# Token mix, transposes and channel product 2 between two tiles: in two half-depth products at the same time instead of in the full array

## The chip, the cores and the metric

One core of one Trainium2 chip. The time is the device time of the kernel in microseconds. TensorE (PE) multiplies, VectorE (DVE) and ScalarE (ACT) read PSUM and compute elementwise, GpSimd (POOL) and SyncE (SP) mostly issue DMAs.

## The reference

A convolution over the last seven tokens with softmax weights for each head, then an MLP over tokens and one over channels, with 8 images of 4096 tokens by 192 channels, all float32:

```python
out = np.einsum('hk,bskhg->bshg', w, x_unf)         # 8 heads, 7 taps, causal
xt = x.transpose(0, 2, 1)
h = np.maximum(xt @ w_tok1, 0.0) @ w_tok2           # tokens: 4096 -> 256 -> 4096
u = x + h.transpose(0, 2, 1)
h2 = np.maximum(u @ w_ch1, 0.0) @ w_ch2             # channels: 192 -> 1536 -> 192
return u + h2
```

## The kernel before

The images are worked in five groups: `[0]`, `[1]`, `[2, 3]`, `[4, 5]`, `[6, 7]`. A group has 8 tiles of 512 tokens (four token blocks of 128). Every float32 operand is split into a high and a low part, and a product is made of three part products (high by high, high by low, low by high). In a group of two images each tile goes through these steps, in the order of the code:

- Channel product 1 of an image (`channel1`, line 926): 192 channels are three columns of 64, so the contraction is 64 deep. Two products with different output features run at the same time, one in array rows 0 to 63, one in rows 64 to 127. A pair takes two PSUM tiles. ScalarE (L965) and VectorE (L966) read both and make `hh` and `hl`, the high and low part of the hidden layer.
- Channel product 2 (`channel2` or `channel2_halves`): the contraction over 1536 hidden features goes in 12 chunks of 128. `channel2` (L1000, L1001) uses all 128 array rows, one PSUM tile for a token block, and VectorE reads it in two adds (L1004, L1005). `channel2_halves` (L983) splits each chunk into rows 0 to 63 and 64 to 127, with a PSUM tile for each half, and VectorE makes four adds that depend on each other (L989, L991).
- Hand-over to the next tile (`turn`), which stands at the last image of the tile only: after its channel product 1 comes the token mix of the next tile (`mix2`, L858 to L860, contraction over 256 hidden tokens, four blocks, one PSUM tile each, added to `u` by VectorE in L873), then half of channel product 2, then the transposes of the mixed tile (`transposed`, L886, three columns, four float32 transposes and one PSUM tile each; ScalarE's L888 and VectorE's L889 make the high and low part in `own`), then the other half of channel product 2. Two copies by ScalarE (L894) and a DMA on POOL's queue (L895) put the other half of the partitions into `other`.

Before the change, images without a hand-over take `channel2_halves`, those with one take `channel2`.

All these products write tiles of the pool `ps_x`, which has six PSUM tiles and hands them out in turn. In this case each tile n waits until tile n − 6 has been read.

The work of the next group (its convolution on VectorE, L636, and its first token product on TensorE, L721 to L723, the background products) is a list of items. The planner `Background` places them between the steps by written costs: `bg.fg(pe, dve, after)` adds the cost of a step on the two engines and then places the items that fit, and while `bg.tiled` is set, no item with TensorE work is placed. There is no other scheduler; each engine runs its instructions in the order of the code.

Of the kernel before, what the change touches and what calls it, by code (L numbers as in the profile page):

```python
# [8 lines left out]
F32 = mybir.dt.float32  # L9
F32R = mybir.dt.float32r  # L10
U32 = mybir.dt.uint32
AF = mybir.ActivationFunctionType
ALU = mybir.AluOpType
AX = mybir.AxisListType

GROUPS = [[0], [1], [2, 3], [4, 5], [6, 7]]
# [98 lines left out]
def conv_mixer_kernel(ctx: ExitStack, tc: tile.TileContext, x, weight, w_tok1, w_tok2, w_ch1, w_ch2, out):  # L115
    nc = tc.nc
    B, S, D = x.shape
# [4 lines left out]
    P = 128  # L122
    NJ = S // P
    KC = JT // P
    NF = FF // P
    D2 = P // 2
    ND = D // D2
    NP = NF // 2
    TJ = 4
    MJ = 2  # L130
    NT = NJ // TJ
    TT = TJ * P
# [5 lines left out]
    def f32(ap):  # L138
        return ap.bitcast(F32)
# [5 lines left out]
    ps_x = ctx.enter_context(tc.tile_pool(name="ps_x", bufs=6, space=bass.MemoryType.PSUM))  # L145
    ps_a = ctx.enter_context(tc.tile_pool(name="ps_a", bufs=1, space=bass.MemoryType.PSUM))
    bg = Background()
# [5 lines left out]
    ident = const.tile([P, P], F32, name="ident")  # L153
# [677 lines left out]
    def rows(v):  # L831
        return v.rearrange("p (c d) -> p c d", d=D2)

    def mix2(gi, q, t2, u, at_once=False):
        nb = len(GROUPS[gi])
        n = nb * D

        def lhs(kc, r, j):
            if gi:
                return t2[:, kc, r, j, :]  # L840
            a0 = ((q % 2) * TJ + j) * P
            return t2s[q // 2][:, kc, r, a0:a0 + P]

        for j in range(TJ):
            ps = ps_x.tile([P, TT], F32, name="ps_x")
            for kc in range(KC):
                a, z = kc == 0, kc == KC - 1
                wh, wl = lhs(kc, 0, j), lhs(kc, 1, j)
                hh, hl = h1[:, kc, 0, :n], h1[:, kc, 1, :n]
                if at_once:  # L850
                    nc.tensor.matmul(out=ps[:, :D], lhsT=wh, rhs=hh, start=a, stop=False)
                    nc.tensor.matmul(out=ps[:, :D], lhsT=wh, rhs=hl, start=False, stop=False)
                    nc.tensor.matmul(out=ps[:, :D], lhsT=wl, rhs=hh, start=False, stop=z)
                elif nb == 1:
                    nc.tensor.matmul(out=ps[:, :2 * D], lhsT=wh, rhs=h1[:, kc, :, :n], start=a, stop=False)  # L855
                    nc.tensor.matmul(out=ps[:, :D], lhsT=wl, rhs=hh, start=False, stop=z)
                else:
                    nc.tensor.matmul(out=ps[:, :n], lhsT=wh, rhs=hh, start=a, stop=False)  # L858
                    nc.tensor.matmul(out=ps[:, :n], lhsT=wh, rhs=hl, start=False, stop=False)  # L859
                    nc.tensor.matmul(out=ps[:, :n], lhsT=wl, rhs=hh, start=False, stop=z)  # L860
            bg.fg(570 if nb == 1 else 1040, 660 if nb == 1 else 600, 200)
            uj = u[:, j]
            one, two = uj[:, :, 1], uj[:, :, 0]
            if at_once:
                nc.vector.tensor_tensor(out=two, in0=rows(ps[:, :D]), in1=one, op=ALU.add)
                nc.scalar.copy(out=one, in_=two)
            elif nb == 1:
                nc.vector.tensor_tensor(out=one, in0=rows(ps[:, :D]), in1=one, op=ALU.add)
                nc.vector.tensor_tensor(out=two, in0=rows(ps[:, D:2 * D]), in1=one, op=ALU.add)
                nc.scalar.copy(out=one, in_=two)  # L870
            else:
                v = ps[:, :n].rearrange("p (b c d) -> p c b d", b=nb, d=D2)
                nc.vector.tensor_tensor(out=uj, in0=v, in1=uj, op=ALU.add)  # L873

    def transposed(gi, u):


        nb = len(GROUPS[gi])
        own = up.tile([P, 2, ND, TT], F32R, name="own")
        low, high = slice(0, D2), slice(D2, P)  # L880

        for c in range(ND):
            ps = ps_x.tile([P, TT], F32, name="ps_x")
            for j in range(TJ):
                cols = u[:, j, c].rearrange("p b d -> p (b d)")
                nc.tensor.transpose(out=ps[:, j * P:(j + 1) * P], in_=cols, identity=ident)  # L886
            bg.fg(440, 600)
            nc.scalar.copy(out=own[:, 0, c], in_=ps)  # L888
            nc.vector.tensor_tensor(out=own[:, 1, c], in0=ps, in1=f32(own[:, 0, c]), op=ALU.subtract)  # L889
        if nb == 1:  # L890
            return [(own, own)]
        other = sp.tile([P, 2, ND, TT], F32R, name="other")
        for k in range(2):
            nc.scalar.copy(out=other[high, k], in_=f32(own[low, k]))  # L894
        nc.gpsimd.dma_start(out=f32(other[low]), in_=f32(own[high]))  # L895
        return [(own, other), (other, own)]

    t2s_of(0)
    up = ctx.enter_context(tc.tile_pool(name="up", bufs=1))
# [16 lines left out]
    def first_transposed():  # L916
        first["abc"] = transposed(0, first["u"][1])
# [189 lines left out]
    def conv_pool(k):  # L1107
        cps[k] = ctx.enter_context(tc.tile_pool(name=f"cp{k}", bufs=1, reuse_waits="tile"))

    def run_ahead(gi):  # L1110

        if gi and gi + 2 < len(GROUPS) and gi + 2 not in starts and bg.idle():
            starts[gi + 2] = stage1(gi + 2, lambda k: cps[k])

    u = None
    starts = {}
    for gi, bs in enumerate(GROUPS):
        nb = len(bs)
        last = gi + 1 == len(GROUPS)
        if gi == 0:  # L1120
            starts[1] = stage1(1, lambda k: sp0)
            starts[1][0](sp0)
            first_items()
        elif not last:
            if gi + 1 not in starts:
                starts[gi + 1] = stage1(gi + 1, lambda k: cps[k])
            starts[gi + 1][0](sp)
        if gi == 0:
            u, abc = first["u"][1], first["abc"]
            loaded = first["next"]  # L1130
        for q in range(NT):
            nxt = (gi, q + 1) if q + 1 < NT else (gi + 1, 0)
            for i, b in enumerate(bs):
                turn = i == nb - 1 and nxt[0] < len(GROUPS)
                run_ahead(gi)
                if turn and nxt[0] != gi:
                    starts[nxt[0]][1]()
                    if gi == 0:
                        stage_ctx.close()
                        t2s_ctx.close()  # L1140
                        conv_pool(1)
                        sp = ctx.enter_context(tc.tile_pool(name="sp1", bufs=1, reuse_waits="tile"))
                    loaded = load_tile(*nxt, sp)
                half = range(0, TJ // 2), range(TJ // 2, TJ)
                ahead = gi or q
                if ahead:
                    h = channel1(abc[i])
                    run_ahead(gi)
                    osb = hp.tile([P, TJ, D], F32, name="osb")
                else:  # L1150
                    osb = first["osb"]
                    first_channel2(u, osb, half[0])
                if turn:
                    if gi == 0 and nxt[0] == 0:
                        bg.require(("t2", nxt[1] // 2, nxt[1] % 2))
                    mix2(*nxt, *loaded)
                    mixed[0] = nxt[1]
                product2 = channel2 if turn or last and q + 1 == NT and i + 1 == nb else channel2_halves
                if ahead:
                    product2(i, h, u, osb, half[0])  # L1160
                if turn:
                    abc = transposed(nxt[0], loaded[1])
                run_ahead(gi)
                if last and q + 1 == NT and i + 1 == nb:
                    for j in range(TJ):
                        if j in half[1]:
                            channel2(i, h, u, osb, [j])
                        store_out(gi, b, q, osb, range(j, j + 1), nc.sync)
                else:
                    if ahead:  # L1170
                        product2(i, h, u, osb, half[1])
                    else:
                        first_channel2(u, osb, half[1])
                    store_out(gi, b, q, osb, range(TJ), nc.gpsimd)
                if not ahead:
                    ht_ctx.close()
                    hp = ctx.enter_context(tc.tile_pool(name="hp", bufs=1, reuse_waits="tile"))
                if turn:
                    u = loaded[1]
                    if nxt[1] + 1 < NT:  # L1180
                        loaded = load_tile(nxt[0], nxt[1] + 1, sp)
# [31 lines left out]
```

## Time and profile before

| | |
|---|---|
| Median of 3 runs | 2077.94 us (2076.01 to 2078.13) |
| Profiled execution | 2075.6 us |
| Its span, first to last instruction | 2073.8 us |
| Granted TensorE clock, mean | 0.996 |
| TensorE busy | 2053.1 us |
| VectorE busy | 1402.8 us |
| ScalarE busy | 761.2 us |

All durations below are of the one profiled execution. A matmul's record shows its start and a modelled end; consecutive matmuls overlap, so the cost of one is read as the step from its start to the start of the next.

### The profile page before, as it was taken

How to read it: one execution, taken by the hardware profiler on the slowest of the kernel's cores; microseconds unless marked ns; L12 is line 12 of the kernel's file. 1: busy time of each engine (PE TensorE's matmuls, PEld its weight loads, DVE VectorE, ACT ScalarE, POOL GpSimd, SP SyncE). 2: the span in 40 equal slices, each digit the busy share in tenths (PEclk: the TensorE clock that was granted, in tenths of full speed). 3: DMA queues.
4: the chain of work that ended last, by engine and by line, in shares of the span. 5: the costliest groups of instructions: out<-in, count | busy, mean ns of one | idle time of the engine just before them, and what ended most of it. 6: DMA issues, size and time to landing. Idle time of an engine off the chain costs nothing.

```text
span 2073.8 us, 41255 instructions
## 1 busy us (share of the span) xinstructions
PE 2053.1 (99%) x17700; PEld 1897.0 (91%) x17700; DVE 1402.8 (68%) x2781; ACT 761.2 (37%) x1305; POOL 101.4 (5%) x167
## 2 busy tenths in 40 slices
PE   9899999999999999999999999999999999999999
PEld 9789899998988999999999999999999999999998
DVE  7899969999549989447965678444455544444444
ACT  4656534434333434224323324232232332233222
POOL 0100000000000000000000000000000000000000
PEclk9999999999999999999999999999999999999999
DMA  9755436544364555243543343322211222222210
GB/s 300 276 159 170 154 119 202 164 150 145 118 173 123 169 166 169 62 112 89 151 116 88 107 123 117 100 77 67 60 48 56 52 62 67 59 67 67 67 32 16
DMA packets 259653, 239.43 MB, mean 115 GB/s; under 512 B 202832, under 2 KB 213584, under 8 KB 257936
## 3 DMA queue, kind: packets, MB, share of 16 engines
q1 hardware_dynamic: 243616, 158.55, 26.8%
q0 software_dynamic: 15856, 78.26, 11.7%
q8 instruction: 139, 2.28, 0.5%
q14 instruction: 42, 0.34, 0.1%
HBM read 146.60 MB, written 71.30 MB: 105 GB/s over the span
## 4 chain that ended last, share of the span: by engine, by line
PE 91%; DVE 6%; DMA 1%; ACT 1%; issue 1%; SPq 0%; ACTq 0%; DVEq 0%
PE ps_x L926 35%; PE ps_x L1000 16%; PE ps_x L983 15%; PE ps_x L1001 7%; PE ps_x L886 2%; DVE xc L636 2%; PE ps_x L858 2%; PE ps_a L721 2%; PE ps_a L722 2%; PE ps_x L860 2%; PE ps_x L859 2%; PE ps_a L723 2%; DVE hl L966 1%; PE ps_a L427 1%; PE ps_x L855 1%; DMA t<-t1d 1%
## 5 line engine op out<-in xcount | busy, mean ns | idle before, releaser
L965 ACT ACTIVATE hh<-ps_x 128x512 fp32r<-128x512 f32 x756 | 410.9, 596 | 810.1 <-PE ps_x L926 810.1
L966 DVE SCALAR_TENSOR_TENSOR hl<-ps_x,hh 128x512 fp32r<-128x512 f32 x756 | 484.7, 684 | 219.4 <-ACT hh L965 218.3
L926 PE MATMUL ps_x<-own,w_hi 64*128 64x512 f32 x2880 | 603.5, 389 | 0.5 <-DVE hl L966 0.3
L1000 PE MATMUL ps_x<-w,hh 128*128 128x384 f32 x1872 | 543.0, 361 | 0.6 <-DVE hl L966 0.6
L926 PEld LDWEIGHTS ps_x<-own,w_hi 64*128 64x128 f32 x2880 | 423.6, 184 | 57.1 <-issue 6.5
L1001 PE MATMUL ps_x<-w,hl 128*128 128x192 f32 x1872 | 468.7, 250 | 0.0
L926 PE MATMUL ps_x<-other,w_hi 64*128 64x512 f32 x1728 | 451.0, 389 | 0.5 <-DVE osb L1005 0.3
L636 DVE SCALAR_TENSOR_TENSOR xc<-raw,cw,xc 128x384 f32<-128x384 f32 (+1 forms) x768 | 388.2, 561 | 8.7 <-ACT xc L634 8.6
L1001 PEld LDWEIGHTS ps_x<-w,hl 128*128 128x128 f32 x1872 | 357.4, 191 | 0.0
L1000 PEld LDWEIGHTS ps_x<-w,hh 128*128 128x128 f32 x1872 | 351.5, 188 | 1.6 <-DVE hl L966 1.4
L926 PEld LDWEIGHTS ps_x<-other,w_hi 64*128 64x128 f32 x1728 | 314.0, 184 | 34.4 <-DVE hl L966 1.8
L983 PE MATMUL ps_x<-w,hh 64*128 64x384 f32 x2304 | 329.9, 355 | 0.0
L926 PE MATMUL ps_x<-own,w_lo 64*128 64x512 f32 x1440 | 323.9, 387 | 0.0
L983 PE MATMUL ps_x<-w,hl 64*128 64x192 f32 x2304 | 292.2, 247 | 0.1
L926 PE MATMUL ps_x<-other,w_lo 64*128 64x512 f32 x864 | 242.1, 386 | 0.0
L926 PEld LDWEIGHTS ps_x<-own,w_lo 64*128 64x128 f32 x1440 | 214.3, 184 | 26.3 <-DVE w_lo L183 0.5
L983 PEld LDWEIGHTS ps_x<-w,hl 64*128 64x128 f32 x2304 | 223.5, 188 | 1.7 <-DVE hl L966 0.8
L983 PEld LDWEIGHTS ps_x<-w,hh 64*128 64x128 f32 x2304 | 219.8, 184 | 0.9
L1004 DVE TENSOR_TENSOR osb<-ps_x,u 128x192 f32<-128x192 f32 x156 | 55.3, 355 | 206.6 <-PE ps_x L1001 206.4
L926 PEld LDWEIGHTS ps_x<-other,w_lo 64*128 64x128 f32 x864 | 159.0, 184 | 17.0
L888 ACT CAST own<-ps_x 128x512 fp32r<-128x512 f32 x120 | 63.3, 594 | 269.4 <-PE ps_x L886 269.4
L991 DVE TENSOR_TENSOR osb<-ps_x,osb 128x192 f32<-128x192 f32 x288 | 102.9, 357 | 17.4 <-DVE osb L991 0.9
(126 smaller groups left out, 1882.5 us busy)
## 6 DMA issues: line engine op xcount, KB each, us to landing
raw<-in_x_dram SPq DMA_DIRECT2D x56, 672.0 KB, 7.0
t<-t2d SPq DMA_DIRECT2D x64, 512.0 KB, 5.1
out_dram<-osb POOLq DMA_DIRECT2D x63, 384.0 KB, 4.7
u<-xcd SPq DMA_DIRECT2D x62, 384.0 KB, 5.7
xcd<-xc POOLq DMA_DIRECT2D x28, 768.0 KB, 7.5
other<-own POOLq DMA_DIRECT2D x24, 768.0 KB, 5.4
t<-t1p SPq DMA_DIRECT2D x32, 512.0 KB, 3.9
t<-t1d SPq DMA_DIRECT2D x32, 256.0 KB, 4.4
```

Source lines behind the costliest of these rows:

```text
L636: nc.vector.scalar_tensor_tensor(out=dst, in0=src, scalar=cw[:, h, k:k + 1], in1=dst, op0=ALU.mult, op1=ALU.add)
L721: nc.tensor.matmul(out=ps, lhsT=wh, rhs=xh, start=a, stop=False)
L722: nc.tensor.matmul(out=ps, lhsT=wh, rhs=xl, start=False, stop=False)
L888: nc.scalar.copy(out=own[:, 0, c], in_=ps)
L926: nc.tensor.matmul(out=ps, lhsT=w1[w][rows, c, p * P:(p + 1) * P], rhs=t[h][rows, v, c], start=n == 0, stop=n == len(prods) - 1,)
L965: nc.scalar.activation(out=h["hh", f], in_=ps, func=AF.Relu)
L966: nc.vector.scalar_tensor_tensor(out=h["hl", f], in0=ps, scalar=0.0, in1=f32(h["hh", f]), op0=ALU.max, op1=ALU.subtract)
L983: nc.tensor.matmul(out=ps[:, :m], lhsT=h[part, f][ks, ts], rhs=w2[ks, f, :m], start=n == 0 and part == "hh", stop=z and part == "hl",)
L991: nc.vector.tensor_tensor(out=osb[:, j], in0=v, in1=osb[:, j], op=ALU.add)
L1000: nc.tensor.matmul(out=ps[:, :2 * D], lhsT=h["hh", f][:, ts], rhs=w2[:, f, :], start=n == 0, stop=False)
L1001: nc.tensor.matmul(out=ps[:, :D], lhsT=h["hl", f][:, ts], rhs=w2[:, f, :D], start=False, stop=z)
L1004: nc.vector.tensor_tensor(out=rows(osb[:, j]), in0=rows(ps[:, :D]), in1=tokens(u, i)[:, j], op=ALU.add)
```

## The change

In a hand-over of a group with two images, the mix, the transposes and both halves of channel product 2 take forms that use the array in two halves of 64 rows, provided that no background product is left in the list at that moment. Where one is left, and in groups of one image, everything stays as it was. The last image of the last tile keeps `channel2`.

```diff
+    def mix2_halves(gi, q, t2, u):
+        nb = len(GROUPS[gi])
+        n = nb * D
+        bg.tiled = True
+        for j in range(TJ):
+            pss = [ps_x.tile([P, TT], F32, name="ps_x") for _ in range(2)]
+            prods = [(kc, w, v) for kc in range(KC) for w, v in ((0, 0), (0, 1), (1, 0))]
+            for k, (kc, w, v) in enumerate(prods):
+                for h, ps in enumerate(pss):
+                    ks = slice(h * D2, (h + 1) * D2)
+                    nc.tensor.matmul(
+                        out=ps[:, :n], lhsT=t2[ks, kc, w, j, :], rhs=h1[ks, kc, v, :n], start=k == 0,
+                        stop=k == len(prods) - 1,
+                    )
+            bg.fg(1040, 1200, 200)
+            for ps in pss:
+                v = ps[:, :n].rearrange("p (b c d) -> p c b d", b=nb, d=D2)
+                nc.vector.tensor_tensor(out=u[:, j], in0=v, in1=u[:, j], op=ALU.add)
+        bg.tiled = False
+
+    def transposed_halves(gi, u):
+        own = up.tile([P, 2, ND, TT], F32R, name="own")
+        low, high = slice(0, D2), slice(D2, P)
+        bg.tiled = True
+        for c in range(ND):
+            pss = [ps_x.tile([P, TT], F32, name="ps_x") for _ in range(2)]
+            for j in range(TJ):
+                for ks, ps in zip((low, high), pss):
+                    cols = u[ks, j, c].rearrange("p b d -> p (b d)")
+                    nc.tensor.transpose(out=ps[:, j * D2:(j + 1) * D2], in_=cols, identity=ident[ks, ks])
+            bg.fg(440, 800)
+            for h, ps in enumerate(pss):
+                v = ps[:, :TJ * D2].rearrange("p (j t) -> p j t", t=D2)
+                hi, lo = (own[:, k, c].rearrange("p (j h t) -> p h j t", h=2, t=D2)[:, h] for k in range(2))
+                nc.scalar.copy(out=hi, in_=v)
+                nc.vector.tensor_tensor(out=lo, in0=v, in1=f32(hi), op=ALU.subtract)
+        bg.tiled = False
+        return shared(own)
...
+                halves = nb > 1 and not (last and q + 1 == NT and i + 1 == nb)
+                if turn and any(it.pe for s in bg.streams for it in s["items"]):
+                    halves = False
...
-                    mix2(*nxt, *loaded)
+                    (mix2_halves if halves else mix2)(*nxt, *loaded)
...
-                product2 = channel2 if turn or last and q + 1 == NT and i + 1 == nb else channel2_halves
+                product2 = channel2_halves if halves else channel2
...
-                    abc = transposed(nxt[0], loaded[1])
+                    abc = (transposed_halves if halves else transposed)(nxt[0], loaded[1])
```

`shared(own)` is the old end of `transposed` (the two copies and the DMA into `other`), moved into a function of its own.

What stands on VectorE in one hand-over of the last group, first before (L873 mix, L1004 and L1005 channel product 2, L889 transposes):

```order
L966 SCALAR_TENSOR_TENSOR hl_18612<-ps_x,hh_18611 128x512 x4
L873 TENSOR_TENSOR u<-ps_x,u 128x384 x4
L1004 TENSOR_TENSOR osb<-ps_x,u 128x192
L1005 TENSOR_TENSOR osb<-ps_x,osb 128x192
L1004 TENSOR_TENSOR osb<-ps_x,u 128x192
L1005 TENSOR_TENSOR osb<-ps_x,osb 128x192
L889 TENSOR_TENSOR own<-ps_x,own 128x512 x3
L1004 TENSOR_TENSOR osb<-ps_x,u 128x192
```

and now (L1011 is the old L966; L893 mix, L1034 and L1036 channel product 2, L912 transposes):

```order
L1011 SCALAR_TENSOR_TENSOR hl_19578<-ps_x,hh_19577 128x512 x4
L893 TENSOR_TENSOR u<-ps_x,u 128x384 x8
L1034 TENSOR_TENSOR osb<-ps_x,u 128x192
L1036 TENSOR_TENSOR osb<-ps_x,osb 128x192 x3
L1034 TENSOR_TENSOR osb<-ps_x,u 128x192
L1036 TENSOR_TENSOR osb<-ps_x,osb 128x192 x3
L912 TENSOR_TENSOR own<-ps_x,own 128x4x64 x6
L1034 TENSOR_TENSOR osb<-ps_x,u 128x192
```

The adds of the mix go from four to eight, those of a block of channel product 2 from two to four, and three subtractions of 512 elements become six of 256.

What TensorE runs around the transposes of a hand-over, with the engines whose signals it waits for, before:

```order
L1001 MATMUL ps_x<-w_463,hl_23456 128x192
L886 MATMUL ps_x<-ident,u 128x128 [waits DMAHW5_49,DMAHW4_49,DVE_49]
L886 MATMUL ps_x<-ident,u 128x128 [waits DVE_49] x3
L886 MATMUL ps_x<-ident,u 128x128 [waits PE_49]
L886 MATMUL ps_x<-ident,u 128x128 x3
L886 MATMUL ps_x<-ident,u 128x128 [waits PE_49]
L886 MATMUL ps_x<-ident,u 128x128 x3
L1000 MATMUL ps_x<-w_463,hh_23451 128x384 [waits PE_49]
```

and now (L906 the transposes, L1028 channel product 2 in halves):

```order
L906 MATMUL ps_x<-ident,u 128x64 [waits DMAHW5_49,DMAHW4_49,DVE_49]
L906 MATMUL ps_x<-ident,u 128x64 [waits DVE_49]
L906 MATMUL ps_x<-ident,u 128x64 x6
L906 MATMUL ps_x<-ident,u 128x64 [waits DVE_49,PE_49]
L906 MATMUL ps_x<-ident,u 128x64 [waits DVE_49]
L906 MATMUL ps_x<-ident,u 128x64 x6
L906 MATMUL ps_x<-ident,u 128x64 [waits DVE_49,PE_49]
L906 MATMUL ps_x<-ident,u 128x64 [waits DVE_49]
L906 MATMUL ps_x<-ident,u 128x64 x6
L1028 MATMUL ps_x<-w_463,hh_17010 128x384 [waits DVE_49] x2
```

Before, the second and third column waited for TensorE itself only, as did the product behind them; now each column and the product behind them waits for a read of VectorE: column 2 for the adds of the block of channel product 2 just ahead of the transposes, the product behind them for the subtractions of column 0.

In two hand-overs of the third group VectorE also has convolution steps (L636) between these, here in the first of them, as it is now:

```order
L893 TENSOR_TENSOR u<-ps_x,u 128x384 x8
L636 SCALAR_TENSOR_TENSOR xc_10857<-raw_10726,cw,xc_10857 128x16x24 x2
L1034 TENSOR_TENSOR osb<-ps_x,u 128x192
L1036 TENSOR_TENSOR osb<-ps_x,osb 128x192 x3
L636 SCALAR_TENSOR_TENSOR xc_10857<-raw_10726,cw,xc_10857 128x16x24 x4
L1034 TENSOR_TENSOR osb<-ps_x,u 128x192
L1036 TENSOR_TENSOR osb<-ps_x,osb 128x192 x3
L912 TENSOR_TENSOR own<-ps_x,own 128x4x64 x6
```

Four steps of the convolution stand between the adds of the two blocks ahead of the transposes.

More of the change, by code (lines that the diff above doesn't have):

```diff
@@ L891, in transposed, with shared @@
             return [(own, own)]
+        return shared(own)
+    def shared(own):
+        low, high = slice(0, D2), slice(D2, P)
         other = sp.tile([P, 2, ND, TT], F32R, name="other")
```

## The prediction

> **What bounds the kernel now.** I read the page first: its busy shares and the chain of work that ended last.
>
> ```profile
> span 2073.8 us, 41255 instructions
> PE 2053.1 (99%) x17700; PEld 1897.0 (91%) x17700; DVE 1402.8 (68%) x2781; ACT 761.2 (37%) x1305; POOL 101.4 (5%) x167
> PE 91%; DVE 6%; DMA 1%; ACT 1%; issue 1%; SPq 0%; ACTq 0%; DVEq 0%
> ```
>
> TensorE (PE) is busy for 99% of the span and carries 91% of the chain, so a microsecond gained or lost on TensorE is one of the kernel. Next the busy time by window, for one steady period of the last group, from one token mix to the next:
>
> ```profile
> 1421.76:1479.44 57.68, 57.68 (x542) 52.95 (x541) 27.98 (x55) 17.46 (x29) 1.64 (x3) 1.00 0.22 60
> ```
>
> The columns are the length, then PE, PEld, DVE, ACT and POOL busy, the granted clock, and DMA. TensorE has no gap in 57.68 us at clock 1.00, and VectorE (DVE) works 27.98 us of them. Then the TensorE timeline through this period (start, length, line, count):
>
> ```profile
> 1400.01 0.36 PE L983 MATMUL ps_x<-w,hh 64*128 64x384 f32 x2
> ...
> 1408.83 0.36 PE L983 MATMUL ps_x<-w,hh 64*128 64x384 f32 x2
> ...
> 1409.32 0.25 PE L983 MATMUL ps_x<-w,hl 64*128 64x192 f32 x2
> 1409.40 0.41 PE L926 MATMUL ps_x<-other,w_hi 64*128 64x512 f32 x1
> ...
> 1409.65 0.39 PE L926 MATMUL ps_x<-other,w_hi 64*128 64x512 f32 x1
> ...
> 1421.44 0.39 PE L926 MATMUL ps_x<-other,w_hi 64*128 64x512 f32 x1
> ...
> 1421.76 0.44 PE L858 MATMUL ps_x<-h,t 128*128 128x384 f32 x1
> 1422.04 0.33 PE L859 MATMUL ps_x<-h,t 128*128 128x384 f32 x1
> 1422.21 0.34 PE L860 MATMUL ps_x<-h,t 128*128 128x384 f32 x1
> ...
> 1425.87 0.33 PE L860 MATMUL ps_x<-h,t 128*128 128x384 f32 x1
> 1426.05 0.33 PE L1000 MATMUL ps_x<-w,hh 128*128 128x384 f32 x1
> ...
> 1426.31 0.36 PE L1000 MATMUL ps_x<-w,hh 128*128 128x384 f32 x1
> 1426.51 0.25 PE L1001 MATMUL ps_x<-w,hl 128*128 128x192 f32 x1
> ...
> 1432.57 0.36 PE L1000 MATMUL ps_x<-w,hh 128*128 128x384 f32 x1
> 1432.76 0.25 PE L1001 MATMUL ps_x<-w,hl 128*128 128x192 f32 x1
> 1432.85 1.47 PE L886 MATMUL ps_x<-ident,u 128*128 128x128 f32 x12
> 1434.08 0.42 PE L1000 MATMUL ps_x<-w,hh 128*128 128x384 f32 x1
> 1434.34 0.25 PE L1001 MATMUL ps_x<-w,hl 128*128 128x192 f32 x1
> ...
> 1440.88 0.25 PE L1001 MATMUL ps_x<-w,hl 128*128 128x192 f32 x1
> 1441.06 0.49 PE L926 MATMUL ps_x<-own,w_hi 64*128 64x512 f32 x1
> ...
> 1441.39 0.39 PE L926 MATMUL ps_x<-own,w_hi 64*128 64x512 f32 x1
> ```
>
> These rows give the steps from start to start. Product 2 in halves (L983) runs 31 chunks from 1400.01 to 1408.83: 0.2845 us a chunk. In the full array (L1000, L1001) it runs 22 from 1426.31 to 1432.57: 0.2845 us too. So two half-depth products at the same time stream no faster than one of full depth, and the change can win only where the array changes its form.
>
> **What it removes.** The planner applies it in 14 hand-overs between tiles (3 in the third group, 4 in the fourth with its last one, 7 in the last group). In each, three small losses go.
> - Channel product 1 into the mix: its pairs step (1421.44 − 1409.65) / 52 = 0.227 us, mix products (1425.87 − 1422.21) / 21 = 0.174. Without a loss the second mix product would start at 1421.44 + 0.227 + 0.174 = 1421.84; it starts at 1422.04. Loss 0.20.
> - Back into product 1: from 1440.88 one L1001 step (0.0875: the chunk's 0.2845 less its first part, 0.197) and one pair step would put the second pair at 1441.20; it is at 1441.39. Loss 0.19, of which the existing hand-over in halves keeps about 0.02 (1409.32 to 1409.65 is 0.33, the two steps 0.31). Gain 0.17.
> - After the transposes, 1434.08 to 1434.34 is 0.26 in place of 0.20 (1426.31 to 1426.51). Gain 0.06.
>
> Together 0.43 us a hand-over. The Trainium skill, TensorEngine Tiling (Array Packing), Key Properties, says that changing the tiling mode drains TensorE; the 0.20 and 0.19 above agree with it. By that rule alone the sum would be the first rival below.
>
> **What it adds.** Half-depth products need two PSUM tiles where one did, and their results are added by VectorE. The pool has six, reused in turn: a pair waits until the pair three before it has been read out. Rows on the readers, VectorE's timeline, then ScalarE's (ACT), then the groups:
>
> ```profile
> 1409.60 0.36 DVE L989 TENSOR_TENSOR osb<-ps_x,u 128x192 f32<-128x192 f32 x1 [1.81 <-PE ps_x L983]
> 1409.99 1.21 DVE L991 TENSOR_TENSOR osb<-ps_x,osb 128x192 f32<-128x192 f32 x3
> ...
> 1422.49 1.29 DVE L966 SCALAR_TENSOR_TENSOR hl<-ps_x,hh 128x512 fp32r<-128x512 f32 x2 [0.75 <-ACT hh L965]
> ...
> 1434.11 1.89 DVE L889 TENSOR_TENSOR own<-ps_x,own 128x512 fp32r<-128x512 f32 x3 [0.30 <-ACT own L888]
> ```
>
> ```profile
> 1433.49 1.57 ACT L888 CAST own<-ps_x 128x512 fp32r<-128x512 f32 x3 [10.54 <-PE ps_x L886]
> ```
>
> ```profile
> L636 DVE SCALAR_TENSOR_TENSOR xc<-raw,cw,xc 128x384 f32<-128x384 f32 (+1 forms) x768 | 388.2, 561 | 8.7 <-ACT xc L634 8.6
> L991 DVE TENSOR_TENSOR osb<-ps_x,osb 128x192 f32<-128x192 f32 x288 | 102.9, 357 | 17.4 <-DVE osb L991 0.9
> L889 DVE TENSOR_TENSOR own<-ps_x,own 128x512 fp32r<-128x512 f32 x120 | 75.9, 684 | 17.4 <-ACT own L888 17.3
> L873 DVE TENSOR_TENSOR u<-ps_x,u 128x384 f32<-128x384 f32 x96 | 51.7, 554 | 39.1 <-PE ps_x L860 39.1
> L476 ACT COPY corner<-ps_x 128x128 f32<-128x128 f32 x2 | 0.5, 266 | 0.0
> L888 ACT CAST own<-ps_x 128x512 fp32r<-128x512 f32 x120 | 63.3, 594 | 269.4 <-PE ps_x L886 269.4
> ```
>
> *Mix.* Streaming stays 6 × 0.174 = 1.05 us per token block, by the equal chunk steps above. VectorE now does two adds a block, the second on the first's result: 0.55 + 0.03 + 0.55 = 1.14 us (0.03 is the gap from 1409.60 + 0.36 to 1409.99). Count from the mix's start, 1421.67. Block 2 takes the tiles of product 1's last pair, read out at 1422.49 + 1.29 = 1423.78, thus at 2.11; TensorE is there at 2.10. Block 0's adds then run 2.11 to 3.25, and block 3 needs them, at 3.21; product 2's first pair needs block 1's, done about 4.39, at 4.35. With 0.03 to 0.05 for each signal, the mix takes 0.05 to 0.20 longer; I take 0.13.
>
> *Transposes.* They stand between two blocks of product 2. Count from their start T; in the rows of product 2 in halves T corresponds to 1409.40. The last block's four adds (L989, L991) end at 1409.99 + 1.21 = 1411.20: T + 1.80. Columns 0 and 1 find free tiles and take 8 × 0.1025 = 0.82 us (12 steps in 1432.85 to 1434.08, 64-row pairs taken at the same step). Column 2 needs the pair of that last block: it waits from T + 0.82 to T + 1.85 with the signal, 1.03 us that nothing hides on TensorE.
> Were a pair's transposes one after the other, columns 0 and 1 would end at T + 1.64, still ahead of T + 1.85; so the unknown step between 0.1025 and 0.205 moves this wait's end by nothing, and the hand-over by 0.02 at most.
>
> *Product 2 after the transposes.* Its next pair takes column 0's tiles, which VectorE leaves last: two subtractions of 256 elements, each 0.42 us (between 357 ns for 192 and 684 for 512), queued behind the four adds. They step as L889's do (three in 1.89), so two take 0.79 and end at T + 2.59; ScalarE's copies of about 0.37 each (between 266 ns for 128 and 594 for 512) are done long before. TensorE is ready at T + 1.85 + 0.41 = T + 2.26: it waits 0.38.
>
> *What else moves.* `other` is filled later, but channel product 1 asks for its first half only after two more blocks, 6.8 us (1434.08 to 1440.88) later, against 0.8 us more of VectorE: covered. The loads on SP's queue and the stores on POOL's keep their places; POOL's copy of `own` waits for the last subtraction, under 1 us later, and its reader is the next image, more than 25 us on. In two hand-overs of the third group VectorE has four convolution steps (L636, 561 ns) between the two blocks' adds: 1.60 + 2.24 = 3.84 us against a block's 12 × 0.2845 = 3.41, so column 2 waits 0.43 more there, 0.8 us in all.
>
> **The sum.** 0.13 + 1.03 + 0.38 − 0.43 = 1.11 us a hand-over; 14 of them 15.5, with the 0.8: +16.3 us. The profiled execution took 2075.6 us (span 2073.8), so it would be 2091.9; the median of the runs, 2077.94, is 2.3 above it, and on that base I predict 2094.
>
> The Trainium skill, TensorEngine Tiling (Array Packing), PSUM Bottleneck, warns that tiling speeds TensorE but not the emptying of PSUM. Taken to its end, a mix bound by VectorE alone, that would be 4 × 1.14 = 4.57 in place of 4.19 us, 0.38 and not 0.13, and 3.5 us more in the sum. By the rows VectorE starts its adds only when TensorE is half done, so the smaller value stays.
>
> **Rivals.**
> - *The removed losses win.* If the adds were out of the way (the four adds read in pairs that free the tiles earlier, the subtractions ahead of them), 14 × −0.43 = −6.0 us: 2072. For it: product 2 in halves followed by product 1 runs without a gap now (1409.32 to 1409.65). Against it: product 1 holds a pair for 2.04 us (9 steps of 0.227), a column of transposes for 0.41, less than the adds' 1.80. It decides if the wait at column 2 falls under 0.4 us. Chance 0.10.
> - *A tie.* Waits of about half the size, say 0.5 us at column 2 and 0.1 after it, would leave 0.1 to 0.3 us a hand-over: +1 to +4 us, 2080. Chance 0.10.
> - *Slower by more.* Subtractions with strided output that cost like 512 elements (0.68), and transposes in halves at 0.205 or more a column step: +0.5 to 1 us a hand-over, 2101 to 2108. No row shows either. Chance 0.10.
>
> **How the numbers follow.** The forecast has 0.70, with a range of its own of 2086 to 2101 (0.55 to 1.65 us a hand-over). Faster by over 0.2% (about what a measurement can tell from no change, 4 us) is the first rival, 0.10; within 0.2% the second, 0.10; slower the forecast and the last, 0.80. The range for 8 in 10 leaves out the faster case below and the top of the last: 2078 to 2104.
>
> **What would show it.** In the new profile: the third column of transposes (L906) starts about 1 us after the second, with VectorE's adds (L1036) as what ended the wait; the first L1028 after it waits for L912; the period goes from 57.7 to about 58.8 us; TensorE's idle time rises by some 20 us. If columns follow each other without a gap, or L906 is long in itself, the step on the transposes is wrong; if the mix (L886) takes over 4.6 us, the one on the mix.

## The result and the profile after

The kernel after took 2092.45 us (median of 6 runs, 2090.64 to 2097.49), the kernel before 2077.35 (6 runs) beside it: a ratio of 1.0076, 95% interval 1.0064 to 1.0087. It is slower by 0.8%; 2094 was forecast, with a range of 2078 to 2104.

The page of the profiled execution (2097.49 us):

```profile
span 2095.7 us, 45328 instructions
PE 2056.8 (98%) x19548; PEld 1940.4 (93%) x19548; DVE 1473.5 (70%) x2991; ACT 764.0 (36%) x1347; POOL 102.2 (5%) x167
PE 90%; DVE 5%; DMA 4%; ACT 1%; SPq 1%; issue 0%; DVEq 0%; ACTq 0%
```

TensorE's idle time, the span less its busy time, went from 20.7 to 38.9 us, a rise of 18.2 where some 20 were named as a sign. VectorE has 70.7 us more work, for 15.1 us of time. This execution was the slowest of the six, and part of its excess is no matter of the change. First and last start of the weight loads of channel product 2 in halves, before (L983) and after (L1028):

```profile
L983 PEld LDWEIGHTS ps_x<-w,hh x2304: 184/184/187, 632.4 to 2043.5; 64*128 64x128 f32 x192
```

```profile
L1028 PEld LDWEIGHTS ps_x<-w,hh x3648: 182/184/188, 638.3 to 2065.4; 64*128 64x128 f32 x192
```

The kernel after comes 5.9 us later to its first product in halves, ahead of every place that the change touches; from there to the end it takes 1427.1 us in place of 1411.1. That is 16.0 us more, near the 15.1 between the medians.

One steady period of the last group, from one token mix to the next, then its stretches (mix, first half of channel product 2, transposes, second half), by window after and before (length, PE, PEld, DVE, ACT, POOL busy, clock, DMA):

```profile
1431.72:1490.44 58.72, 57.84 (x673) 57.14 (x671) 32.94 (x71) 17.75 (x32) 1.64 (x3) 1.00 0.23 60
1431.72:1436.01 4.29, 4.29 (x51) 4.12 (x47) 3.33 (x7) 1.09 (x2) 0.00 (x0) 1.00 0.00 0
1436.01:1442.89 6.88, 6.88 (x98) 6.75 (x98) 3.56 (x9) 0.00 (x0) 0.00 (x0) 1.00 0.46 155
1442.89:1445.17 2.28, 1.40 (x29) 1.15 (x25) 1.81 (x6) 1.20 (x4) 0.00 (x0) 1.00 0.00 0
1445.17:1452.24 7.07, 7.07 (x99) 6.92 (x96) 3.03 (x9) 3.50 (x4) 0.53 (x1) 1.00 0.54 115
```

```profile
1421.67:1426.05 4.38, 4.38 (x27) 4.29 (x25) 2.86 (x6) 1.09 (x2) 0.00 (x0) 1.00 0.00 0
1426.05:1432.85 6.80, 6.80 (x49) 6.80 (x49) 1.27 (x3) 0.00 (x0) 0.00 (x0) 1.00 0.45 157
1432.85:1434.08 1.23, 1.23 (x14) 1.23 (x13) 0.71 (x2) 0.59 (x2) 0.00 (x0) 1.00 0.00 0
1434.08:1441.06 6.98, 6.98 (x51) 6.82 (x50) 2.60 (x5) 3.83 (x4) 0.53 (x1) 1.00 0.54 113
```

The period went from 57.68 (the row in the prediction) to 58.72 us. Over ten periods, before and then after, it grew by 1.06 us on average:

```profile
1421.76:1998.56 576.80, 576.80 (x5403) 529.50 (x5401) 280.76 (x552) 175.34 (x292) 16.41 (x30) 1.00 0.22 60
```

```profile
1431.72:2019.16 587.44, 578.29 (x6722) 566.94 (x6720) 330.82 (x703) 178.19 (x322) 16.41 (x30) 1.00 0.22 60
```

The stretch of the transposes alone took 2.28 in place of 1.23, and in it TensorE was busy for only 1.40. The wait, in the timelines of TensorE and VectorE (the bracket is the idle time and what ended it):

```profile
1442.89 0.28 PE L906 MATMUL ps_x<-ident,u 64*128 64x64 f32 x2
...
1443.01 0.71 PE L906 MATMUL ps_x<-ident,u 64*128 64x64 f32 x14
1444.08 0.24 PE L906 MATMUL ps_x<-ident,u 64*128 64x64 f32 x1 [0.36 <-DVE osb L1036]
1444.84 0.46 PE L906 MATMUL ps_x<-ident,u 64*128 64x64 f32 x7 [0.52 <-DVE osb L1036]
1445.17 0.77 PE L1028 MATMUL ps_x<-w,hh 64*128 64x384 f32 x2
1445.51 0.35 PE L1028 MATMUL ps_x<-w,hl 64*128 64x192 f32 x1
```

```profile
1443.18 0.36 DVE L1034 TENSOR_TENSOR osb<-ps_x,u 128x192 f32<-128x192 f32 x1 [1.81 <-PE ps_x L1028]
1443.57 1.21 DVE L1036 TENSOR_TENSOR osb<-ps_x,osb 128x192 f32<-128x192 f32 x3
1444.70 1.41 DVE L912 TENSOR_TENSOR own<-ps_x,own 128x256 fp32r<-128x256 f32 x4
```

Sixteen transposes (columns 0 and 1) run through. The first of column 2 comes when two of VectorE's four adds are done (1444.08), the other seven when the fourth is (1443.57 + 1.21 = 1444.78; 1444.84). Over all 14 hand-overs the group says the same:

```profile
L906 PE MATMUL ps_x<-ident,u 64*128 64x64 f32 x336 | 20.1, 227 | 13.1 <-DVE osb L1036 13.1
```

### The profile page after: what moved, and what is told of

It reads as the page before. It is cut to its first block, busy times and chain, and to the rows that moved or that the text cites. A ratio compares the mean times of both kernels' runs of the same rounds, so it can differ in the third digit from the quotient of the medians.

```text
span 2095.7 us, 45328 instructions
## 1 busy us (share of the span) xinstructions
PE 2056.8 (98%) x19548; PEld 1940.4 (93%) x19548; DVE 1473.5 (70%) x2991; ACT 764.0 (36%) x1347; POOL 102.2 (5%) x167
## 4 chain that ended last, share of the span: by engine, by line
PE 90%; DVE 5%; DMA 4%; ACT 1%; SPq 1%; issue 0%; DVEq 0%; ACTq 0%
PE ps_x L971 36%; PE ps_x L1028 24%; PE ps_x L1045 11%; PE ps_x L1046 5%; PE ps_x L886 3%; PE ps_a L721 2%; PE ps_a L722 2%; PE ps_a L723 2%; PE ps_x L927 1%; DVE xc L636 1%; PE ps_x L855 1%; DMA dec_raw<-in_moe_w_ch_dram 1%; DVE osb L1036 1%; DMA t<-t1d 1%; PE ps_a L717 1%; PE ps_x L858 1%
## 5 line engine op out<-in xcount | busy, mean ns | idle before, releaser
L1011 DVE SCALAR_TENSOR_TENSOR hl<-ps_x,hh 128x512 fp32r<-128x512 f32 x756 | 485.1, 685 | 199.4 <-ACT hh L1010 198.1
L1028 PE MATMUL ps_x<-w,hh 64*128 64x384 f32 x3648 | 534.2, 357 | 0.0
L1028 PE MATMUL ps_x<-w,hl 64*128 64x192 f32 x3648 | 510.9, 248 | 0.1
L1028 PEld LDWEIGHTS ps_x<-w,hh 64*128 64x128 f32 x3648 | 457.4, 184 | 4.5
L1028 PEld LDWEIGHTS ps_x<-w,hl 64*128 64x128 f32 x3648 | 457.6, 188 | 1.2 <-DVE hl L1011 0.8
L636 DVE SCALAR_TENSOR_TENSOR xc<-raw,cw,xc 128x384 f32<-128x384 f32 (+1 forms) x768 | 388.8, 561 | 8.7 <-ACT xc L634 8.7
L1045 PE MATMUL ps_x<-w,hh 128*128 128x384 f32 x1200 | 349.6, 362 | 0.6 <-DVE hl L1011 0.6
L1046 PE MATMUL ps_x<-w,hl 128*128 128x192 f32 x1200 | 300.6, 251 | 0.0
L1046 PEld LDWEIGHTS ps_x<-w,hl 128*128 128x128 f32 x1200 | 229.6, 191 | 0.0
L1045 PEld LDWEIGHTS ps_x<-w,hh 128*128 128x128 f32 x1200 | 225.8, 188 | 1.5 <-DVE hl L1011 1.4
L1034 DVE TENSOR_TENSOR osb<-ps_x,u 128x192 f32<-128x192 f32 x152 | 54.1, 356 | 210.4 <-PE ps_x L1028 210.4
L1036 DVE TENSOR_TENSOR osb<-ps_x,osb 128x192 f32<-128x192 f32 x456 | 163.1, 358 | 26.4
L1049 DVE TENSOR_TENSOR osb<-ps_x,u 128x192 f32<-128x192 f32 x100 | 35.4, 354 | 85.6 <-PE ps_x L1046 85.3
```

What stands on the lines that cost most here:

```text
L636: nc.vector.scalar_tensor_tensor(out=dst, in0=src, scalar=cw[:, h, k:k + 1], in1=dst, op0=ALU.mult, op1=ALU.add)
L1011: nc.vector.scalar_tensor_tensor(out=h["hl", f], in0=ps, scalar=0.0, in1=f32(h["hh", f]), op0=ALU.max, op1=ALU.subtract)
L1028: nc.tensor.matmul(out=ps[:, :m], lhsT=h[part, f][ks, ts], rhs=w2[ks, f, :m], start=n == 0 and part == "hh", stop=z and part == "hl",)
L1034: nc.vector.tensor_tensor(out=rows(osb[:, j]), in0=rows(pss[0][:, :D]), in1=tokens(u, i)[:, j], op=ALU.add)
L1036: nc.vector.tensor_tensor(out=osb[:, j], in0=v, in1=osb[:, j], op=ALU.add)
L1045: nc.tensor.matmul(out=ps[:, :2 * D], lhsT=h["hh", f][:, ts], rhs=w2[:, f, :], start=n == 0, stop=False)
```

## Experiments

Theory A: the time is lost where TensorE waits for PSUM tiles that VectorE has not yet read. Theory B: the products in halves, or the doubled work on VectorE, cost it themselves. The kernels below ran in two sets, each beside the kernel before on the same chip (2078.02 us in the first set, 2076.88 in the second).

**The columns of the transposes apart.** One column behind each of the first three blocks of channel product 2:

```diff
-    def transposed_halves(gi, u):
-
-        own = up.tile([P, 2, ND, TT], F32R, name="own")
+    def transposed_halves(gi, u, own=None, cs=range(ND)):
+
+        whole = own is None
+        if whole:
+            own = up.tile([P, 2, ND, TT], F32R, name="own")
...
-        for c in range(ND):
+        for c in cs:
...
-                if ahead:
+                spread = turn and halves
+                if spread:
+                    own = up.tile([P, 2, ND, TT], F32R, name="own")
+                    for j in range(ND):
+                        product2(i, h, u, osb, range(j, j + 1))
+                        transposed_halves(nxt[0], loaded[1], own, range(j, j + 1))
+                    abc = shared(own)
+                elif ahead:
...
-                        product2(i, h, u, osb, half[1])
+                        product2(i, h, u, osb, range(ND, TJ) if spread else half[1])
...
```

> Kernel after, but one column of the transposes behind each of the first three blocks of channel product 2, instead of all three columns behind the second block; the same instructions otherwise. Theory A (the loss is TensorE waiting for PSUM tiles that VectorE has not read): every pair of tiles is now asked for a whole block (3.4 us) after its last use, so no wait is left at the transposes; per hand-over -0.43 us for the switches, +0.10 for the mix, about -0.2 for transposes that step at 0.08 instead of 0.10 us: about -0.5 us against before, 14 times: 2070 us (2066 to 2074), 22 below the kernel after. Theory B (the products in halves, or the doubled VectorE work, cost the time themselves, wherever they stand): 2092 us as after.

Measured: 2070.85 us, ratio to before 0.9962 (0.9949 to 0.9976). The same instructions (45328 in both pages), in another order, are 7 us faster than before and about 22 faster than the kernel after. Its period, and its transposes (L908):

```profile
1424.01:1481.06 57.05, 57.05 (x675) 56.75 (x672) 33.01 (x71) 17.83 (x32) 1.64 (x3) 1.00 0.23 61
```

```profile
L908 PE MATMUL ps_x<-ident,u 64*128 64x64 f32 x336 | 23.7, 220 | 0.0
```

From a column's first transpose to the product behind it, TensorE's timeline has 0.22 us:

```profile
1431.82 0.22 PE L908 MATMUL ps_x<-ident,u 64*128 64x64 f32 x1
...
1432.04 0.41 PE L1030 MATMUL ps_x<-w,hh 64*128 64x384 f32 x1
```

The idle time ahead of the transposes is 0.0 in place of 13.1 us, with VectorE as busy as in the kernel after (33.01 against 32.94 us a period). Theory B falls: forms and work are all there.

**Transposes back in the full array.**

```diff
-                    abc = (transposed_halves if halves else transposed)(nxt[0], loaded[1])
+                    abc = transposed(nxt[0], loaded[1])
```

> Kernel after with the transposes alone put back into the full array (one tile a column), mix and channel product 2 in halves. Theory A: single tiles find tiles that have been read, the waits of 1.0 and 0.3 us go; the two switches at channel product 1 are saved (-0.37), two new ones stand around the transposes (+0.40), the mix costs +0.10: about +0.1 us a hand-over against before, 2079 us (2076 to 2083). Theory B: most of the loss stays, 2088 to 2092 us.

Measured: 2081.65 us, ratio 1.0020 (1.0011 to 1.0029). Most of the loss is gone, as A says, but it ends 3.6 us above before, not 1. Its period, then its first half of channel product 2 and its transposes:

```profile
1427.02:1484.97 57.95, 57.95 (x663) 56.43 (x661) 32.77 (x68) 17.46 (x29) 1.64 (x3) 1.00 0.22 61
```

```profile
1431.29:1438.43 7.14, 7.14 (x99) 6.85 (x97) 3.57 (x9) 0.00 (x0) 0.00 (x0) 1.00 0.42 149
1438.43:1439.89 1.46, 1.46 (x14) 1.29 (x12) 1.21 (x4) 0.76 (x2) 0.00 (x0) 1.00 0.00 0
```

No idle time shows in the period, which is 0.27 us longer than before's. The transposes, with a change of form on each side, take 1.46 us in place of 1.23, and the first half of channel product 2 takes 7.14 in place of 6.80 (see the last section); that is more than the hand-over saves elsewhere.

**Only the mix in halves.**

```diff
-                product2 = channel2_halves if halves else channel2
+                product2 = channel2_halves if halves and not turn else channel2
...
-                    abc = (transposed_halves if halves else transposed)(nxt[0], loaded[1])
+                    abc = transposed(nxt[0], loaded[1])
```

> Only the token mix of the hand-over in halves, transposes and channel product 2 as before. The two switches stay, the first moves behind the mix. Theory A: only the mix's small waits are left, +0.1 us a hand-over: 2079 us (2077 to 2082). Theory B in the form that the mix's doubled adds on VectorE are the cost: 2088 to 2092 us.

Measured: 2083.66 us, ratio 1.0025 (1.0014 to 1.0035). This missed on the high side by 2 us.

```profile
1426.31:1484.38 58.07, 58.07 (x567) 54.53 (x564) 30.01 (x60) 17.47 (x29) 1.64 (x3) 1.00 0.22 60
```

The period is 0.39 us longer than before's. Some 0.27 of it is the mix with the change of form now behind it: from the mix's start to the second chunk of channel product 2 it is 4.91 us (1426.31 to 1431.22) in place of 4.64 (1421.67 to 1426.31). The rest is again a slower first half of channel product 2. It is no 1.06: the mix's doubled adds aren't the loss.

**Two adds in place of four ahead of the transposes.**

```diff
-    def channel2_halves(i, h, u, osb, js):
+    def channel2_halves(i, h, u, osb, js, adds=4):
...
-            for v in (pss[0][:, D:2 * D], pss[1][:, :D], pss[1][:, D:2 * D]):
+            for v in (pss[0][:, D:2 * D], pss[1][:, :D], pss[1][:, D:2 * D])[1 if adds == 2 else 0:2 if adds == 2 else 3]:
...
-                    product2(i, h, u, osb, half[0])
+                    if turn and halves:
+                        channel2_halves(i, h, u, osb, half[0], adds=2)
+                    else:
+                        product2(i, h, u, osb, half[0])
```

> Kernel after, but in the hand-overs the two blocks of channel product 2 ahead of the transposes are read by two of the four adds (one for each PSUM tile; the other two partial products are left out of the output). TensorE does the same. Theory A: VectorE is free 0.78 us earlier, the third column and the product behind the transposes start that much earlier: 14 x 0.78 = 11 us less than after, 2081 us (2078 to 2084). Theory B (TensorE's own cost): 2092 us as after.

Measured: 2082.71 us, ratio 1.0024 (1.0014 to 1.0033). Above before it is 4.7 us, where the kernel after is 15.1: 10.4 us went with 28 pairs of adds, on an engine that is idle for almost half of the period.

```profile
1423.54:1481.43 57.89, 57.70 (x674) 57.09 (x672) 31.56 (x67) 17.65 (x32) 1.64 (x3) 1.00 0.22 61
```

```profile
L906 PE MATMUL ps_x<-ident,u 64*128 64x64 f32 x336 | 19.3, 228 | 3.0 <-DVE osb L1036 3.0
```

The period shown is 0.83 us shorter than the kernel after's; over ten periods (580.12 us in place of 587.44) it is 0.73, where 0.78 was expected. The wait ahead of the transposes falls from 13.1 to 3.0 us.

**Two pairs of PSUM tiles in place of three.** Columns 0 and 1 share a pair, and both are read behind column 1:

```diff
         for c in range(ND):
-            pss = [ps_x.tile([P, TT], F32, name="ps_x") for _ in range(2)]
+            a = c % 2 * TJ * D2
+            if not a:
+                pss = [ps_x.tile([P, TT], F32, name="ps_x") for _ in range(2)]
...
-                    nc.tensor.transpose(out=ps[:, j * D2:(j + 1) * D2], in_=cols, identity=ident[ks, ks])
+                    nc.tensor.transpose(out=ps[:, a + j * D2:a + (j + 1) * D2], in_=cols, identity=ident[ks, ks])
...
+            if c == 0:
+                continue
...
```

> Kernel after, with the first two columns of the transposes in one pair of PSUM tiles: two pairs in place of three, all three columns still behind the second block of channel product 2. The instructions on TensorE, VectorE and ScalarE are the same. Theory A (waiting for PSUM tiles to be read): the three columns now run without a wait (about 1.0 us), and the next block of channel product 2 is what waits for the four adds, until 1.85 us after the start of the transposes; nothing waits behind it. Per hand-over 1.85 in place of 2.28, and the 0.2 to 0.3 us behind it gone: 14 x -0.67 = -9 us against after: 2083 us (2080 to 2087). Rival (it is the position between two blocks, or the transposes in halves as such): 2092 us.

Measured: 2085.25 us, ratio 1.0036 (1.0023 to 1.0050). It is 8.4 us above before in place of 15.1, so 6.7 went where 9 were expected. The wait moved as expected. TensorE's timeline around it, the group of the transposes (L908), and who waits for the four adds (L1041; L1033 is channel product 2):

```profile
1434.16 0.28 PE L908 MATMUL ps_x<-ident,u 64*128 64x64 f32 x2
...
1434.27 0.95 PE L908 MATMUL ps_x<-ident,u 64*128 64x64 f32 x22
...
1435.33 0.41 PE L1033 MATMUL ps_x<-w,hh 64*128 64x384 f32 x1
1436.09 0.44 PE L1033 MATMUL ps_x<-w,hh 64*128 64x384 f32 x1 [0.36 <-DVE osb L1041]
```

```profile
L908 PE MATMUL ps_x<-ident,u 64*128 64x64 f32 x336 | 15.2, 222 | 0.0
```

```profile
PEld ps_x L1033 <- DVE osb L1041: 8.5, 14, 0.6
```

All 24 transposes run without a wait. The next block starts one half behind them (1435.33) and the other when the adds are done, 1.93 us after the transposes' start (1.85 expected). The wait follows the tile and not the instruction.

**Channel product 2 always in the full array**, from the kernel before; it prices the gain.

```diff
-                product2 = channel2 if turn or last and q + 1 == NT and i + 1 == nb else channel2_halves
+                product2 = channel2
```

> Kernel before, with channel product 2 in the full array for the 24 images without a hand-over too: two changes of the array's form more in each of them, half of the adds on VectorE. It measures the gain that the change was credited with. If a change of form costs the 0.20 and 0.17 us read from the rows of before: 24 x 0.37 = +9 us, 2087 us (2084 to 2090). If it costs nothing on the whole: 2078 us.

Measured: 2085.49 us, ratio 1.0041 (1.0028 to 1.0053). That is 8.6 us for 24 images, 0.36 us (0.24 to 0.46) for two changes of form, where 0.37 was read from the rows. Background products may now stand in these images as well. In the last group there is none, and the steady period there says the same:

```profile
1426.33:1484.43 58.10, 58.10 (x446) 52.89 (x444) 25.13 (x47) 17.46 (x29) 1.65 (x3) 1.00 0.22 60
```

It is 0.42 us longer than the 57.68 of before, for the two changes of form of one image.

**Only the transposes in halves.**

```diff
-                    (mix2_halves if halves else mix2)(*nxt, *loaded)
+                    mix2(*nxt, *loaded)
...
-                product2 = channel2_halves if halves else channel2
+                product2 = channel2_halves if halves and not turn else channel2
```

> Only the transposes of the hand-over in halves, mix and channel product 2 in the full array. Theory A: two more changes of form (+0.40), transposes stepping at 0.08 (-0.2), and the third column waits for two adds in place of four (about 0.15): +0.35 us a hand-over, 2083 us (2080 to 2086). Rival (transposes in halves are the cost of the change, wherever they stand): 2090 us or more.

Measured: 2083.06 us, ratio 1.0027 (1.0018 to 1.0036). With two adds ahead of the transposes (L1050, of the full form) in place of four, the wait is a quarter of the kernel after's:

```profile
L906 PE MATMUL ps_x<-ident,u 64*128 64x64 f32 x336 | 16.8, 230 | 3.4 <-DVE osb L1050 3.4
```

## Why the prediction was right

- *The sum.* 1.11 us a hand-over were forecast, 1.06 were measured in the last group; 14 of them make 14.9 of the 15.1 us between the medians. In the period shown, the terms are 0.19 for the mix (0.13 forecast), 1.05 for the transposes (1.03) and 0.24 behind them (0.38), taking the 0.43 saved as forecast. So the transposes are the loss, as forecast. That the sum came so close is in part luck, since the errors of the two smaller terms partly cancel.
- *The wait at column 2.* Forecast to last until T + 1.85; the seven transposes that need both tiles came at T + 1.95 in the period shown, and the stretch took 2.28 where the steps gave 2.26. In ten of the 14 hand-overs they came at T + 1.86 and the stretch took 2.19, behind a first half of channel product 2 of 7.00 in place of 6.88:

```profile
1553.53:1560.53 7.00, 7.00 (x99) 6.87 (x98) 3.56 (x9) 0.00 (x0) 0.00 (x0) 1.00 0.42 152
1560.53:1562.72 2.19, 1.27 (x28) 1.01 (x24) 1.81 (x6) 1.20 (x4) 0.00 (x0) 1.00 0.00 0
```

```profile
1562.39 0.46 PE L906 MATMUL ps_x<-ident,u 64*128 64x64 f32 x7 [0.52 <-DVE osb L1036]
```

Less waiting work on VectorE (two adds), another assignment of tiles (two pairs) and another place of the columns each move the time as this wait says: shown. The columns themselves were mis-sized: apart from each other they take about 0.22 us, not 0.41. For the first two it mattered to nothing, since the adds' end sets the time; column 2 took 0.33 behind the wait, which in the period shown nearly made up for the wait's 0.10.
- *The wait behind the transposes.* Forecast 0.38. By the step of 0.2845, 24 chunks are 6.83 us; the second half of channel product 2 took 7.07, 0.24 more. The profile puts down no wait of L1028 for L912, which had been named as a sign, but the starts agree with it:

```profile
1444.70 0.74 DVE L912 TENSOR_TENSOR own<-ps_x,own 128x256 fp32r<-128x256 f32 x2
```

These are the subtractions of column 0. One takes 0.41, so they end at 1445.11 and 1445.44, and the two halves of the next block start their first product at 1445.17 and 1445.50 (two products in 0.77 from 1445.17, one of 0.44), each 0.06 later. The forecast counted until both tiles were read, T + 2.59 (it was T + 2.55). That one half could start its first product 0.33 before the other is the likely reason that the term was too large; this was not tested apart.
- *The mix.* Forecast 0.13 more, less the 0.20 of the change of form: 4.31; measured 4.29, against 4.38. But part of its cost came just behind it: the first half of channel product 2 took 6.88 in place of 6.80, so that the two together lost 0.19 in the period shown, and 0.31 where that half took 7.00.
- *The gain.* 0.37 us for two changes of form, measured by the kernel in the full array at 0.36 by the medians and 0.42 by the steady period.
- *The convolution's steps.* Forecast 0.43 us more in two hand-overs. In both of them column 2's seven transposes come 2.16 us after the first, 0.2 to 0.3 more than in the others; here the first. Their periods, which were 57.68 before, are 0.35 and 0.60 us above those of the last group, so the two together cost some 0.95 where 0.8 was forecast, not all of it at column 2.

```profile
1001.26 0.28 PE L906 MATMUL ps_x<-ident,u 64*128 64x64 f32 x2
...
1003.42 0.46 PE L906 MATMUL ps_x<-ident,u 64*128 64x64 f32 x7 [0.52 <-DVE osb L1036]
```

```profile
990.06:1049.15 59.09, 58.00 (x674) 53.19 (x672) 54.54 (x114) 20.65 (x38) 3.46 (x5) 1.00 0.40 113
1049.15:1108.49 59.34, 58.24 (x675) 55.85 (x672) 45.93 (x97) 19.51 (x36) 3.47 (x5) 1.00 0.45 128
```

The first rival, that the saved changes of form win, is what happens once the wait is gone: forecast at 2072, measured with the columns apart at 2070.85. Quicker transposes (0.22 us a column in place of 0.41) add to what is saved there; the rival did not count them.

Of the warning in the Trainium skill, TensorEngine Tiling (Array Packing), PSUM Bottleneck, the trace agrees with the kind of the loss (TensorE waits for reads of PSUM), but not with an engine that is full: VectorE is busy for 32.94 of 58.72 us. It is the order of the reads that costs, in one place.

## What to carry to other kernels

When a product is split into two partial sums, count the PSUM tiles between a product and its reuse, and ask when the last of its reads ends, not how busy the reading engine is. Short steps with tiles of their own (transposes here) belong one at a time between long ones, so that each pair of tiles has a long step's time to be read. A saving that a bad place hides may be had by moving the step: the same instructions went from 0.8% slower to 0.4% faster.

## What the runs showed that was not expected

- The two halves of the array need not run in step. In the kernel after, the half whose tile is free first starts 0.33 us ahead (1445.17, 1445.50), and in the following blocks the two stay apart: one keeps 0.2845 us a chunk (23 chunks from 1445.70 to 1452.24), the other takes 0.290 (22 from 1445.87 to 1452.25).
- In the two kernels with a mix in halves and transposes in the full array, the first half of channel product 2 ran slower than before (7.14 and 7.05 us in place of 6.80), with no idle time shown. With only the mix in halves:

```profile
1431.22 0.37 PE L1045 MATMUL ps_x<-w,hh 128*128 128x384 f32 x1
...
1437.60 0.37 PE L1045 MATMUL ps_x<-w,hh 128*128 128x384 f32 x1
```

These are 22 chunks in 6.38 us, 0.290 a chunk against 0.2845 before, at the same granted clock of 1.00. After the transposes the step is 0.285 again. It accounts for about 2 of the 5.6 us of that kernel. The cause is open, here and for the step of 0.290 above.
